# The key maxima of the next pair of heads, queued later on VectorE in a three-stage attention, expert and mixer kernel

## The chip, the cores and the metric

The kernel runs as one program on one core of a Trainium2 chip. The metric is the device time of the whole launch in microseconds (us), as a median of runs. Five engines work from queues of their own, each in the order in which its instructions stand: PE (TensorE, with PEld for its weight loads), DVE (VectorE), ACT (ScalarE), POOL (GpSimd) and SP (SyncE, which issues the loads and stores here). They wait for one another by semaphores.

## The reference, cut to what matters

Three stages follow each other, for two batches of 768 positions:

```python
# stage 1: attention, 8 heads of 64, over a window and over 24 block summaries
k_sum = k.reshape(B, H, nb, block, D).max(axis=3)      # key maxima of blocks of 32
v_sum = v.reshape(B, H, nb, block, D).mean(axis=3)
scores_l = np.where(mask_l, scale * q @ k.T, -1e9)     # |i - j| < 16
scores_s = scale * einsum(q, k_sum) + np.log(block)
a = softmax(concat(scores_l, scores_s)); attn = a @ concat(v, v_sum)
...
# stage 2: four experts of causal attention (q, k, v by x @ w), the best two per position weighted
# stage 3: mixer over positions (w_tok1, w_tok2), then over channels
h2 = np.maximum(u @ w_ch1, 0.0) @ w_ch2                # 512 -> 1536 -> 512
return u + h2
```

The mixer's weights come as 64-bit floats and are decoded on the chip.

## The kernel before, in words

**Stage 1, batch by batch, pair by pair.** Heads go in pairs (`hp`, four a batch), a pair's 768 positions in three groups `g` of four tiles of 64 queries. `s1_load` loads a pair's keys `kx` (already cut into windows, with 24 free columns a tile for the key maxima), its queries `qb`, its values `vt` and `vx`. `s1_keys` makes the key maxima: a reduction on DVE (L185, tile `km`) and a copy into `kx` (L187). Per group, PE multiplies the scores (`s1_scores`, L217, tile `s1s`), DVE takes the minima of the negated scores (`s1_minima`, L227, tiles `n` and `mn`, four pairs of instructions), ACT exponentiates (L236), POOL and DVE normalise (L240, L244, L252), PE turns the result (L257), ACT copies it out (L262), PE multiplies by the values (L271), and ACT and DVE split the result into a high and a low part (L279, L282). Scores of four tiles take a bank of PSUM; there are three banks of that kind, and a bank comes free when the minima have read it. `sc`, `km` and the others have numbers in an order listing: `s1s102` is batch 1, pair 0, group 2; `kx11` is batch 1, pair 1.

**What sets the order.** Batch 0's stage 1 follows a list written out by hand. Batch 1's (the function `s1`) is written in a loop, and a scheduler places its instructions on each engine, with its own estimate of times, among those that it may run with. `tc.issue_after(x)` keeps what is issued under it behind instruction `x` in its engine's queue, and `last["mn", b, hp, g]` is the last minimum of that group. Both queries buffers serve two pairs in turn, so that the loads of pair `hp + 2` are issued when pair `hp`'s scores are done.

**Around it.** Beside batch 1's stage 1 run the projections of batch 0 (`proj`, tiles `pv`, `pj`, V), then the experts' attention (`attn`: L476 scores, L481 minima, L486 exponentials, L492 the multiplication on POOL, L502 turns, L507 to L513 values), the token mixer (`tokmix`, whose last step makes `u`, split into `u0h` and `u0l`), and the decoding of the mixer's weights (`decode_w`, L140 to L153: a load into one of two buffers `raw`, and steps on ACT, POOL and DVE; tile names `raw`, `deca`, then `t1`, `t2`, `c1`, `c2` with h for high and l for low). The channel mixer (`chmix`, tiles `h` and `o`) takes the second half of the time in four passes; the first needs `u` of batch 0 and the first six decoded channel tiles (`c1` and `c2`, three each).

Of the kernel before, what the change touches and what calls it, by code (L numbers as in the profile page):

```python
# [53 lines left out]
def stack_kernel(ctx: ExitStack, tc, qT, kT, kwT, vw, vT, wqkv, wo, tok1, tok2, ch1, ch2,  # L54
# [4 lines left out]
    last = {}  # L59
# [96 lines left out]
    def s1_load(b, hp, qb):  # L156
        first = b == 0 and hp == 0
        kx = unit([P, NT, KX], F32, f"kx{b}{hp}")
        kt = None
        if first:  # L160

            kt = kt0
            vec.memset(kx[:, 0, KW:KX], 0.0)

        vt = half([P, S], F32, "vt") if b else None
        vx = unit([P, NT, P], F32, f"vx{b}{hp}")
        loads = [(kt, kT) if first else (kx, kwT[b, hp])]
        loads += [(qb[i::2, :, i, :], qT[b, hp, i::2].rearrange("p (t c) -> p t c", c=P)) for i in range(2)]
        if first:
            loads += [(lmask, lmask_d), (ident, ident_d), (blocks, blocks_d)]  # L170
        loads += ([(vt, vT[b, hp])] if b else []) + [(vx[:KW], vw[b, hp])]
        for d, src in loads:
            if b == 0:
                r = tc.keep_in_program_order(nc.sync.dma_start(d, src))
            else:
                with tc.issue_after(last["load"].ins):
                    r = nc.sync.dma_start(d, src)
        last["load"] = r
        return kt, vt, kx, vx

    def s1_keys(kt, vt, kx, vx):
        km = sp1.tile([P, NBLK], F32, name="km")
        sums = (kx[:, :, KW:KX], km[:, None, :].broadcast_to([P, NT, NBLK]))
        if kt is None:
            vec.tensor_reduce(km.rearrange("p (t n) -> p t n", t=NT),  # L185
                              kx[:, :, WIN:WIN + TQ].rearrange("p t (n c) -> p t n c", c=BLK), axis=AX.X, op=ALU.max)
            vec.tensor_copy(*sums)  # L187
            return
        vec.tensor_reduce(km, kt[:, WIN:WIN + S].rearrange("p (n c) -> p n c", c=BLK), axis=AX.X, op=ALU.max)
        kc = kt[:, :S].rearrange("p (t c) -> p t c", c=TQ)  # L190
        w = 4
        for t in range(0, NT, w):
            u = min(t + w, NT - 1)
            vec.tensor_copy(kx[:, t:t + w, 0:TQ], kc[:, t:t + w])
            vec.tensor_copy(kx[:, t:u, TQ:KW], kc[:, t + 1:u + 1, 0:2 * WIN])
            if t + w == NT:
                vec.tensor_copy(kx[:, NT - 1, TQ:KW], kt[:, S:S + 2 * WIN])
            if t == 0:
                vec.tensor_copy(*sums)
# [13 lines left out]
    def s1_scores(b, hp, g, qb, kx):  # L213
        sc = bank("sc", f"s1s{b}{hp}{g}")
        for i in range(4):
            t = 4 * g + i
            ten.matmul(sc[:, KX * i:KX * i + KX], qb[:, t // 2].rearrange("p i c -> p (i c)")[:, t % 2::2], kx[:, t, :],  # L217
                       start=True, stop=True)
        return sc
# [19 lines left out]
    def s1_sm(sm):  # L239
        gps.tensor_scalar(sm, sm, 1e-9, 1.0, op0=ALU.add, op1=ALU.mult)  # L240

    def s1_ri(sm):
        ri = sp1.tile([P, 4], F32, name="ri", bufs=4)
        vec.reciprocal(ri, sm)  # L244
        return ri
# [106 lines left out]
    def s1(xh, xl, qbs):  # L352

        b = 1
        n = 3 * HP
        nq = len(qbs)
        lds = [s1_load(b, 0, qbs[0])]
        ex, pTs, av = {}, {}, {}
        with tc.issue_after(last["mn", 0, HP - 1, 2].ins):
            s1_keys(*lds[0])  # L360
        for i in range(n + 4):
            hp, g = divmod(i, 3)
            if i < n:
                sc = s1_scores(b, hp, g, qbs[hp % nq], lds[hp][2])
                ex[i] = s1_exps(*s1_minima(b, hp, g, sc))
                if g == 0 and len(lds) < min(hp + 2, HP):
                    lds.append(s1_load(b, hp + 1, qbs[(hp + 1) % nq]))
            if 0 <= i - 1 < n:
                pr, sm = ex[i - 1]
                s1_sm(sm)  # L370
                s1_mul(b, pr, s1_ri(sm))
            if i < n and g == 1:
                with tc.issue_after(last["mn", b, hp, 0].ins):
                    vs = s1_sums(*lds[hp])
                s1_means(b, hp, vs, lds[hp][3])
                if hp + 1 < HP:
                    s1_keys(*lds[hp + 1])
            if 0 <= i - 2 < n:
                pTs[i - 2] = s1_turned(s1_turn(b, *divmod(i - 2, 3), ex[i - 2][0]))
            if 0 <= i - 4 < n:  # L380
                s1_low(*divmod(i - 4, 3), av[i - 4], xh, xl)
            if 0 <= i - 3 < n:
                hp, g = divmod(i - 3, 3)
                av[i - 3] = s1_values(b, hp, g, lds[hp][3], pTs[i - 3])
                s1_high(hp, g, av[i - 3], xh)
            if i < n:
                yield
# [275 lines left out]
    lds = []  # L663
# [127 lines left out]
```

## Time and profile before

| | |
|---|---|
| median of 3 runs | 469.67 us (468.07 to 472.2) |
| the profiled execution's own time | 467.73 us |
| its span | 465.9 us |
| PE busy | 445.1 us (96%) |
| DVE, ACT, POOL busy | 280.1, 231.2, 285.2 us |
| granted TensorE clock, mean | 0.998 of full speed |

The profiled execution took 1.83 us more than its span and lies 1.94 us below the median of the runs. Busy times are sums over stages that differ: what a stage is limited by is read from the idle time of the engines in that stage and from what ended it.

### The profile page before, as it was taken

The numbers are of one execution on the slowest core, as the hardware profiler recorded it, in microseconds if no ns is written. First come the engines' busy times: TensorE is split into PE (matmuls) and PEld (weight loads), VectorE is DVE, ScalarE is ACT, GpSimd is POOL, SyncE is SP. The second block draws the span as 40 slices with busy tenths as digits, with TensorE's granted clock in tenths as the row PEclk, the third lists the DMA queues.
The fourth block names the chain that finished last, engine by engine and source line by source line (L and its number), as shares of the span: only waits on it lengthen the run. The fifth ranks groups of instructions, "written<-read, shape, count | busy, mean of one in ns | idle before, by whom it ended". The sixth has DMA issues, their size and how long they took to land.

```text
span 465.9 us, 8565 instructions
## 1 busy us (share of the span) xinstructions
PE 445.1 (96%) x3038; PEld 420.7 (90%) x3038; DVE 280.1 (60%) x818; ACT 231.2 (50%) x653; POOL 285.2 (61%) x319
## 2 busy tenths in 40 slices
PE   7899899999989878999999999999999999999996
PEld 7798789989978766897999999999999999999996
DVE  5573766759699679868773743677572673332322
ACT  4685665977778687885664423233323321111010
POOL 4568542768989887997873869877864771000000
PEclk9999999999999999999999999999999999999999
DMA  7999917806515865021111120212121100001111
GB/s 222 275 255 310 289 39 207 182 2 167 127 46 152 210 171 146 3 91 45 45 47 46 66 70 2 84 53 78 58 91 45 62 32 0 1 0 69 68 70 68
DMA packets 28522, 46.51 MB, mean 100 GB/s; under 512 B 2496, under 2 KB 19648, under 8 KB 28480
## 3 DMA queue, kind: packets, MB, share of 16 engines
q1 hardware_dynamic: 28480, 45.97, 35.2%
q8 instruction: 24, 0.39, 0.4%
q14 instruction: 18, 0.15, 0.1%
HBM read 33.38 MB, written 3.15 MB: 78 GB/s over the span
## 4 chain that ended last, share of the span: by engine, by line
PE 68%; DMA 10%; DVE 7%; POOL 4%; ACT 3%; issue 3%; SPq 3%; DVEq 0%; ACTq 0%; POOLq 0%
PE h L113 7%; PE h L112 7%; PE h L114 7%; PE o L112 7%; PE o L113 7%; PE o L114 7%; DMA kx<-in_kwT_dram 5%; PE s1s L217 4%; PE s1a L271 2%; DMA qb<-in_qT_dram 2%; POOL pr L492 2%; PE u L112 2%; PE pj L112 2%; PE u L113 2%; PE u L114 2%
## 5 line engine op out<-in xcount | busy, mean ns | idle before, releaser
L144 POOL TENSOR_SCALAR deca<-deca 128x512 f32<-128x512 f32 x30 | 58.0, 1938 | 10.5 <-ACT deca L143 9.7
L113 PE MATMUL o<-hl,c2h 128*128 128x384 f32 x192 | 64.2, 337 | 0.0
L114 PE MATMUL o<-hh,c2l 128*128 128x384 f32 x192 | 64.0, 336 | 0.0
L108 ACT ACTIVATE hh<-h 128x384 fp32r<-128x384 f32 x48 | 23.3, 490 | 79.4 <-PE h L114 78.8
L109 DVE SCALAR_TENSOR_TENSOR hl<-h,hh 128x384 fp32r<-128x384 f32 x48 | 26.5, 555 | 53.2 <-ACT hh L108 53.2
L605 DVE TENSOR_TENSOR oa<-o,oa 128x384 f32<-128x384 f32 x64 | 31.9, 550 | 38.5 <-PE o L114 38.5
L112 PE MATMUL o<-hh,c2h 128*128 128x384 f32 x192 | 49.4, 336 | 0.0
L236 ACT ACTIVATE pr<-n,mn 128x120 f32<-128x120 f32 x96 | 36.6, 384 | 16.3 <-DVE mn L227 15.8
L150 POOL TENSOR_TENSOR raw<-raw 128x512 f32<-128x512 f32 x30 | 31.3, 1042 | 20.4 <-DVE raw L147 18.6
L492 POOL TENSOR_SCALAR pr<-pr,f,wg 128x128 f32<-128x128 f32 (+5 forms) x48 | 40.1, 849 | 5.1 <-DVE f L489 2.9
L151 POOL TENSOR_TENSOR deca<-deca,raw 128x512 f32<-128x512 f32 x30 | 40.8, 1360 | 1.0
L149 ACT ACTIVATE raw<-raw 128x512 f32<-128x512 uint32 x30 | 20.3, 677 | 36.3 <-DMA raw<-in_ch_dram 25.6
L145 DVE TENSOR_SCALAR deca<-deca 128x512 int32<-128x512 int32 x30 | 27.8, 928 | 14.9 <-POOL deca L144 14.9
L486 ACT ACTIVATE pr<-pr,mn 128x128 f32<-128x128 f32 (+5 forms) x48 | 31.9, 665 | 9.8 <-DVE mn L481 9.7
L113 PEld LDWEIGHTS o<-hl,c2h 128*128 128x128 f32 x192 | 36.0, 188 | 0.3 <-DVE hl L109 0.3
L114 PEld LDWEIGHTS o<-hh,c2l 128*128 128x128 f32 x192 | 36.0, 188 | 0.0
L112 PEld LDWEIGHTS o<-hh,c2h 128*128 128x128 f32 x192 | 34.8, 188 | 0.1
L113 PE MATMUL h<-u0l,c1h 128*128 128x384 f32 x96 | 32.5, 338 | 0.0
L112 PE MATMUL h<-u0h,c1h 128*128 128x384 f32 x96 | 32.4, 338 | 0.0
L114 PE MATMUL h<-u0h,c1l 128*128 128x384 f32 x96 | 32.3, 337 | 0.0
L112 PE MATMUL h<-u1h,c1h 128*128 128x384 f32 x96 | 32.3, 336 | 0.0
L113 PE MATMUL h<-u1l,c1h 128*128 128x384 f32 x96 | 32.3, 336 | 0.0
(207 smaller groups left out, 1315.1 us busy)
## 6 DMA issues: line engine op xcount, KB each, us to landing
raw<-in_ch_dram SPq DMA_DIRECT2D x24, 512.0 KB, 3.5
kx<-in_kwT_dram SPq DMA_DIRECT2D x7, 720.0 KB, 10.0
vx<-in_vw_dram SPq DMA_DIRECT2D x8, 576.0 KB, 11.1
qb<-in_qT_dram SPq DMA_DIRECT2D x16, 192.0 KB, 8.9
raw<-in_tok_dram SPq DMA_DIRECT2D x6, 512.0 KB, 4.6
out_dram<-oa SPq DMA_DIRECT2D x16, 192.0 KB, 2.0
vt<-in_vT_dram SPq DMA_DIRECT2D x4, 384.0 KB, 10.3
rqk<-in_wqkv_dram SPq DMA_DIRECT2D x4, 256.0 KB, 10.2
```

What stands on the lines that cost most here:

```text
L109: vec.scalar_tensor_tensor(lo, src, 0.0, hi.bitcast(F32), op0=ALU.max, op1=ALU.subtract)
L112: ten.matmul(out, lh, rh, start=start, stop=False)
L113: ten.matmul(out, lh, rl, start=False, stop=False)
L114: ten.matmul(out, ll, rh, start=False, stop=stop)
L144: gps.tensor_scalar(af, af, F64_TINY, F64_HUGE, op0=ALU.max, op1=ALU.min)
L145: vec.tensor_scalar(ta, ta, 3, 0x3FFFFFFF, op0=ALU.logical_shift_left, op1=ALU.bitwise_and)
L150: gps.tensor_mul(lf, lf, ef)
L151: gps.tensor_add(af, af, lf)
L236: act.activation(pr[:, i, :], n[:, i, :], AF.Exp, bias=mn[:, i:i + 1], scale=-1.0, accum_out=sm[:, i:i + 1])
L486: act.activation(prs[r], prs[r], AF.Exp, bias=mn[:, r, ci:ci + 1], scale=-1.0, accum_out=sm[:, r:r + 1])
L492: gps.tensor_scalar(prs[r][:, :nk], prs[r][:, :nk], f[:, r:r + 1], wg[:, 3 * h + r, e:e + 1], op0=ALU.mult, op1=ALU.mult)
L605: vec.tensor_add(oa[d], a[:, :HALF], oa[d])
```

## The change: where the key maxima of the next pair may stand

In batch 1, `s1_keys` of the next pair is issued in the middle of a pair's second group. It was free to stand anywhere in DVE's queue from there; now its reduction and its copy are kept behind the last minimum of the second group of the pair at work. Nothing is added or taken away, and the first pair of batch 1 has a call of its own, which is as it was.

```diff
                 s1_means(b, hp, vs, lds[hp][3])
                 if hp + 1 < HP:
-                    s1_keys(*lds[hp + 1])
+                    with tc.issue_after(last["mn", b, hp, 1].ins):
+                        s1_keys(*lds[hp + 1])
```

Since the scheduler places everything by estimated times, the order of later work moves too. Lines after L376 have numbers higher by one in the changed kernel.

DVE, batch 1, pair 0 (`s1s100` and `s1s101` are the scores of its groups 0 and 1, `kx11` the keys of pair 1, `wqk1l` a weight of the projections):

```order
 L244 RECIPROCAL ri_622<-sm_602 128x4
-L185 TENSOR_REDUCE km_833<-kx11_749 128x24
 L227 ISA n_737,mn_738<-s1s100_732,lmask_77 128x120
...
 L227 ISA n_807,mn_808<-s1s101_802,lmask_77 128x120
 L227 ISA mn_808 128x1
+L185 TENSOR_REDUCE km_833<-kx11_749 128x24
 L126 TENSOR_TENSOR wqk1l_114<-rqk1_118,wqk1h_113 128x256 x3
+L187 COPY kx11_749<-km_833 128x12x24
```

The reduction of pair 1's keys stood ahead of the minima of groups 0 and 1 of pair 0, and stands behind both now. The same holds for pairs 2 and 3 (`kx12` goes from ahead of the minima of pair 1's groups 0 and 1 to behind both, `kx13` from ahead of group 1's of pair 2 to behind them).

POOL, in the experts' attention of batch 1, between the multiplications of the third expert's first half (`pr384_2983`) and second half (`pr512_3085`); `deca_2813`, `deca_2966` and `deca_3070` are the second, third and fourth channel tile in decoding. Before:

```order
L492 TENSOR_SCALAR pr384_2983<-pr384_2983,f2_2980,wg_1961 128x384
L151 TENSOR_TENSOR deca_2966<-deca_2966,raw64_2965 128x512
L150 TENSOR_TENSOR raw64_3069<-raw64_3069 128x512
L488 TENSOR_SCALAR sm2_3083<-sm2_3083 128x3
L153 TENSOR_TENSOR c1l0_2730<-deca_2966,c1h0_2729 128x512
L151 TENSOR_TENSOR deca_3070<-deca_3070,raw64_3069 128x512
L492 TENSOR_SCALAR pr512_3085<-pr512_3085,f2_3084,wg_1961 128x512
```

The same place on POOL in the changed kernel:

```order
L493 TENSOR_SCALAR pr384_2983<-pr384_2983,f2_2980,wg_1961 128x384
L144 TENSOR_SCALAR deca_2966<-deca_2966 128x512
L151 TENSOR_TENSOR deca_2813<-deca_2813,raw64_2812 128x512
L489 TENSOR_SCALAR sm2_3083<-sm2_3083 128x3
L153 TENSOR_TENSOR c1l0_2730<-deca_2813,c1h0_2729 128x512
L493 TENSOR_SCALAR pr512_3085<-pr512_3085,f2_3084,wg_1961 128x512
```

At this multiplication the decoding of the channel weights stands one tile further back than before: six of its POOL steps (L144 once, L150 twice, L151 twice, L153 once) that stood ahead of `pr512_3085` stand behind it.

SP, at the load of the second channel tile (`raw64_2812`; the `k211` and `k2l11` rows are the copies of the experts' keys of batch 1, which wait for the last projection). Before:

```order
L140 DMA raw64_2733<-in_ch1_dram 128x4x256
L140 DMA raw64_2812<-in_ch1_dram 128x4x256
L449 DMA k211_2253<-s111h_2394 64x768
L450 DMA k211_2253<-s111h_2394 64x768
L453 DMA k2l11_2254<-s111l_2395 64x768 x2
```

And in the changed kernel:

```order
L140 DMA raw64_2733<-in_ch1_dram 128x4x256
L450 DMA k211_2253<-s111h_2394 64x768
L451 DMA k211_2253<-s111h_2394 64x768
L454 DMA k2l11_2254<-s111l_2395 64x768 x2
L450 DMA k211_2253<-s111h_2394 64x768
L451 DMA k211_2253<-s111h_2394 64x768
L454 DMA k2l11_2254<-s111l_2395 64x768 x2
L140 DMA raw64_2812<-in_ch1_dram 128x4x256
```

The second channel tile's load has gone behind the eight copies of keys.

## Rows read from the trace of the kernel before

**Rows 1.** Chain of waits: start us, us, what

```profile
36.42 9.97 DMA kx<-in_kwT_dram
```

**Rows 2.** DVE's instructions in order of time, 46 to 63 us

```profile
46.41 0.95 DVE L185 TENSOR_REDUCE km<-kx 128x24 f32<-128x768 f32 x1 [5.82 <-DMA kx<-in_kwT_dram]
47.28 0.27 DVE L227 CUSTOM_DVE_ANT_0 n<-s1s,lmask 128x120 f32<-128x120 f32 x1
...
48.95 0.30 DVE L187 COPY kx<-km 128x288 f32<-128x288 f32 x1
...
51.26 0.27 DVE L227 CUSTOM_DVE_ANT_0 n<-s1s,lmask 128x120 f32<-128x120 f32 x1
...
62.43 0.95 DVE L185 TENSOR_REDUCE km<-kx 128x24 f32<-128x768 f32 x1 [1.49 <-DMA kx<-in_kwT_dram]
```

**Rows 3.** PE's instructions in order of time, 40 to 84 us

```profile
40.97 1.20 PE L217 MATMUL s1s<-kx,qb 128*128 128x120 f32 x8
...
44.85 1.09 PE L217 MATMUL s1s<-kx,qb 128*128 128x120 f32 x8
48.23 0.50 PE L217 MATMUL s1s<-kx,qb 128*128 128x120 f32 x2 [2.29 <-DVE mn L227]
...
54.02 0.73 PE L217 MATMUL s1s<-kx,qb 128*128 128x120 f32 x4 [0.36 <-DVE mn L227]
...
60.62 0.38 PE L217 MATMUL s1s<-kx,qb 128*128 128x120 f32 x2
...
64.64 1.20 PE L217 MATMUL s1s<-kx,qb 128*128 128x120 f32 x8 [0.95 <-DVE mn L227]
...
75.51 1.09 PE L217 MATMUL s1s<-kx,qb 128*128 128x120 f32 x8
...
79.79 1.09 PE L217 MATMUL s1s<-kx,qb 128*128 128x120 f32 x8
...
83.58 0.39 PE L217 MATMUL s1s<-kx,qb 128*128 128x120 f32 x2
```

**Rows 4.** Stretches: busy PE, PEld, DVE, ACT, POOL; clock, DMA share, GB/s

```profile
36.00:48.00 12.00, 9.94 (x106) 8.76 (x104) 3.97 (x15) 5.20 (x22) 10.48 (x17) 1.00 1.05 304
48.00:64.00 16.00, 15.09 (x175) 14.02 (x175) 10.46 (x49) 10.22 (x44) 6.95 (x17) 1.00 0.78 219
...
250.00:300.00 50.00, 50.00 (x287) 49.48 (x287) 25.17 (x43) 17.71 (x34) 40.39 (x33) 1.00 0.13 43
```

**Rows 5.** The sum of the stretches from 102 to 230 us

```profile
sum 128.00, PE 118.68 PEld 104.24 DVE 105.31 ACT 97.66 POOL 111.88; mean PE 9.13 PEld 8.02 DVE 8.10 ACT 7.51 POOL 8.61
```

**Rows 6.** Loads issued at 35.24 and 74.45 us: KB, us to landing

```profile
vt<-in_vT_dram SPq DMA_DIRECT2D x1, 384.0 KB, 7.1
...
kx<-in_kwT_dram SPq DMA_DIRECT2D x1, 720.0 KB, 6.0
```

**Rows 7.** POOL's decoding steps by line: count, busy us, mean ns, idle before

```profile
L144 POOL TENSOR_SCALAR deca<-deca 128x512 f32<-128x512 f32 x30 | 58.0, 1938 | 10.5 <-ACT deca L143 9.7
...
L150 POOL TENSOR_TENSOR raw<-raw 128x512 f32<-128x512 f32 x30 | 31.3, 1042 | 20.4 <-DVE raw L147 18.6
...
L151 POOL TENSOR_TENSOR deca<-deca,raw 128x512 f32<-128x512 f32 x30 | 40.8, 1360 | 1.0
```

**Rows 8.** DVE's decoding steps by line, 100 to 240 us: same columns

```profile
L146 DVE SCALAR_TENSOR_TENSOR deca<-raw,deca 128x512 int32<-128x512 int32 x14 | 12.2, 869 | 0.1
...
L145 DVE TENSOR_SCALAR deca<-deca 128x512 int32<-128x512 int32 x14 | 10.1, 721 | 2.8 <-POOL deca L144 2.8
...
L147 DVE TENSOR_SCALAR raw<-deca 128x512 int32<-128x512 int32 x14 | 8.8, 627 | 0.0
```

**Rows 9.** Tile `c2l`: ns min/median/max, first and last start, shapes

```profile
L114 PEld LDWEIGHTS o<-hh,c2l x192: 187/188/192, 243.1 to 461.5; 128*128 128x128 f32 x192
...
L153 POOL TENSOR_TENSOR c2l<-deca,c2h x12: 1284/1297/1418, 208.9 to 385.7; 128x512 fp32r<-128x512 f32 x12
```

**Rows 10.** POOL in order of time: the third `c2l` step of the first six tiles

```profile
228.49 1.28 POOL L153 TENSOR_TENSOR c2l<-deca,c2h 128x512 fp32r<-128x512 f32 x1
```

## The prediction

> **What bounds the kernel now.** I read the stretches first: how long PE stands idle in each, since from 250 to 300 us it works without a pause [rows 4], and the end moves by what the time before that loses or wins. From 36 to 64 us, about the stretch that the change touches, PE is idle for 2.06 + 0.91 = 2.97 us of 28 [rows 4]; from 102 to 230 us for 9.32 of 128 [rows 5]. So PE is nearly the bound there already. Then PE in order of time: three pauses, 2.29, 0.36 and 0.95 us, the last from 63.69 to 64.64, make up all of it (2.29 + 0.36 + 0.31 up to 64), and each ended with a minimum on DVE [rows 3]. Then DVE in order of time, for why the minima were late: from 40.6 to 46.41 us it waited 5.82 us for the keys of pair 1, with nothing left ahead of that pair's key maxima; only then came the minima of pair 0's group 0, whose scores PE had finished at 40.97 + 1.20 = 42.17 us [rows 2, 3]. The chain of waits shows the same load, 9.97 us long, as a piece of its own [rows 1]. The reader is to see a wait for something needed later that stands in front of something needed now.
>
> **The 2.29 us pause.** Moved behind the minima of group 1, the reduction no longer holds group 0 back: its minima start at 42.2 instead of 47.28 us. They read the scores and free a bank of PSUM at about 43, before PE finishes group 1's scores at 45.94 [rows 3], so PE goes on with group 2 at once. Does another wait take over? Next on DVE stands a sum over `vt`, loaded at 35.24 us and landed 7.1 us later, at 42.3 [rows 6]: no wait. From the first minimum of group 0 to that of group 1 DVE took 3.98 us [rows 2]; started at 42.2, it comes to group 1 at 46.2, just after its scores, and four minima of 0.27 us end at 47.0 to 47.3. The reduction follows, and its keys landed at 46.41 [rows 2]: it waits for nothing. Sum: -2.29 us.
>
> **The 0.36 and 0.95 us pauses.** Both are waits for minima that stood behind the same stall or behind the next one. The second is pair 1's: its group 0 minima stood behind the reduction of pair 2's keys, which waited 1.49 us and started at 62.43 [rows 2]; PE needed their bank at 63.69 and got it at 64.64 [rows 3]. After the change PE reaches that point 2.65 us sooner, at 61.04; group 0's last scores, 60.62 + 0.38 before, are done at 58.35, and four minima later it is 59.4. Both pauses go: -1.31 us.
>
> **What is late next.** The loads of pair 2 are issued when pair 0's scores are done, and in the new order two of the last four products stand further back on PE, so that these loads leave at about the time they left before. Nor would leaving sooner help: the DMA share is 1.05 from 36 to 48 us [rows 4], so a load joins a full line. I leave `kx12` landing at 62.4. Its reduction now stands behind pair 1's group 1 minima: PE starts those scores at 61.04, they take 1.20, minima 1.1, so it starts at 63.3 and waits for nothing. The first user, pair 2's group 0, is at 75.5 before, 71.9 then [rows 3]: the reduction (0.95 us) and its copy have over 7 us of cover. Pair 3 is the tight one. Its load follows the copies of the projections, which PE brings 3.6 us sooner; 6.0 us of landing [rows 6] puts the keys at 76.9 instead of 80.4. The reduction then waits for pair 2's group 1: scores 79.79 + 1.09 - 3.6 = 77.3, minima to 78.2, reduction to 79.2, copy (0.30 [rows 2]) to 79.5; PE wants the keys at 83.58 - 3.6 = 80.0 [rows 3]. The cover there is 0.5 us, and every microsecond beyond it would be a microsecond on PE. I cost it at nothing. Sum of the stage: **-3.6 us**.
>
> **What is carried to the end.** PE, POOL, DVE and ACT all start the next stage that much sooner, and no load there stands at a fixed time. But the scheduler has also dealt the work from 102 to 230 us anew, and that stretch is mixed: PE 93%, POOL 87%, DVE 82% busy [rows 5]. Two moves bear on it, both counted in instructions that stand ahead of something that PE needs.
> - Decoding of the channel weights goes back. Ahead of the first split of `u`, with which the channel mixer's stretch begins, one tile's three DVE steps less: 0.72 + 0.87 + 0.63 = 2.2 us [rows 8]; ahead of a later one, two tiles' (4.4) less and one step of 0.5 more, net 3.9. On POOL 1.94 + 2 x 1.04 + 2 x 1.36 + 1.30 = 8.0 us less ahead of the multiplication shown [rows 7, 9]. The gain's end: 3.9, what DVE gives up, since the split needs DVE whatever POOL does.
> - In batch 0's attention it goes the other way: ahead of the third expert's first minima, one decoding tile's DVE steps (2.2) and seven smaller ones, some 1.8 us by their neighbours, come in. The loss's end: +4.0.
>
> No row shows how such moves come out: work taken out from ahead of a step shortens its wait only while its engine is what it waits for. I take **-0.9 us**, 40% of the 2.2 at the first split, nearer to the gain because that place is the last one before PE is full. Total -4.5 us, with ends of -3.6 - 3.9 = -7.5 and -3.6 + 4.0 = +0.4.
>
> **A rule on how much room there is.** The room that I read from PE's busy time, 9.3 us from 102 to 230 us, is a ceiling on what the second stage can give [rows 5]. The Trainium skill, "Perfetto Trace Analysis", section "Identifying the Most-Contended Engine", says that matmul busy time is no good measure of how near TensorE is to its limit, since matmuls are pipelined, and that the busy share of weight loads is to be used. By that measure the room there is 128 - 104.24 = 23.8 us; the trace bears the rule out, for in the full stretch the weight loads are busy for 49.48 of 50 us [rows 4, 5]. By that measure the first rival below would be nowhere near the ceiling: its 3.9 us are 42% of the 9.3, and 16% of the 23.8.
>
> **Rivals.**
> - *The second stage gains in full.* Everything that DVE gives up at the later split of `u` is gained: -3.6 - 3.9 = -7.5 us, 462.2 us as a median. For it: decoding stood between attention's steps on all three engines and needs only to be ready for the channel mixer. Against: batch 0's attention gets decoding in front.
> - *The gain is given back.* Attention of batch 0 meets its 4.0 us on DVE, or pair 3's keys are late, and the 3.6 us are spent by 230 us: 467 to 471, say 469.7 us. This is also what would come if the stall only changed its name, so that DVE waits for a landing behind another instruction.
> - *Slower: the channel tiles come too late.* Their decoding has gone back, and the second tile's load has gone behind eight copies. Before, the third low half of `c2` was ready at 228.49 + 1.28 = 229.8 us, and PE took up the first at 243.1 [rows 9, 10], 13.3 us of cover; with PE 4.5 us sooner it is 8.8. The three came from 208.9 to 228.5, 9.8 us apart [rows 9, 10]. One place back costs 9.8 and is nearly all covered; 8.0 us of POOL is 1.4 tiles of 5.6; at two places the tile is ready at 249.4 where PE wants it at 238.6, a wait of 10.8 against a gain of 4.5: +6.3, 476.0 us. It decides from 8.8 us of delay and ends slower than before from 13.3. Against it: the next six tiles keep their place on POOL, so the first six have to catch up before them.
>
> **How the numbers follow.** The profiled execution took 467.73 us; less 4.5 that is 463.2. The median of the runs is 1.94 above it, so I forecast 469.67 - 4.5 = **465.2 us** as a median. About 1% (4.7 us) is what a measurement of this kernel can tell from no change; the forecast lies just inside. Chances: the forecast, -2.5 to -5.5 us, 0.45; the full gain, beyond -5.5, 0.25; given back, -2.5 to +1.5, 0.20; slower, beyond that, 0.10. Faster by over 1% is all of the second and somewhat under a third of the first: 0.38. Slower by over 1% is some half of the last: 0.06. Between: 0.56. For 8 times in 10 the range leaves out the slower case and the far end of the full gain: -8.2 to +1.2 us, 461.5 to 470.9.
>
> **What would show it.** Right: the wait of L185 for the keys is gone from DVE for pairs 1 to 3, or falls, for pairs 1 and 2 together, from 7.3 us (5.82 + 1.49) to under 1; PE has no pause at a score product between 45 and 65 us; the third group of pair 2 and what follows on PE stand 3.6 us earlier. The second stage is right if PE's idle time from 102 to 230 us, shifted, falls by a microsecond or so. Wrong: a pause of PE of over 0.5 us before pair 3's scores; a wait for `vt` on DVE; PE waiting for `c2l`; or PE's idle time growing after 102 us by as much as it fell before.

## The result, and the profile after

The changed kernel is slower: 471.94 us (20 runs) against 468.79 (20 runs of the kernel before on the same chip). The ratio is 1.0071 with a 95% interval of 1.0049 to 1.0094, so 3.3 us (2.3 to 4.4) more. I had forecast 4.5 us less. The profiled execution took 473.46 us, its span is 471.7, the mean granted clock 0.978; the 20 runs granted 0.973 to 0.996. The ratios here and below are of undisturbed executions, and km_rest, whose profiled execution was a disturbed one, has no row in the table of starts and no line of its trace shown.

What the edit aims at came about. VectorE's instructions in order of time in the changed kernel, the three key maxima of pairs 1 to 3 with a minimum ahead and two copies:

```profile
49.38 0.27 DVE L227 CUSTOM_DVE_ANT_0 n<-s1s,lmask 128x120 f32<-128x120 f32 x1
...
49.58 0.94 DVE L185 TENSOR_REDUCE km<-kx 128x24 f32<-128x768 f32 x1
...
52.35 0.30 DVE L187 COPY kx<-km 128x288 f32<-128x288 f32 x1
...
64.94 0.95 DVE L185 TENSOR_REDUCE km<-kx 128x24 f32<-128x768 f32 x1
...
80.04 0.95 DVE L185 TENSOR_REDUCE km<-kx 128x24 f32<-128x768 f32 x1
81.02 0.78 DVE L187 COPY kx<-km 128x288 f32<-128x288 f32 x1
```

The waits of 5.82 and 1.49 us in front of the first two [rows 2] are gone: none of the three has a bracket. The stretches of the same kernel (busy PE, PEld, DVE, ACT, POOL, then granted clock, DMA share, GB/s):

```profile
36.00:48.00 12.00, 12.00 (x138) 10.77 (x135) 7.74 (x32) 8.19 (x34) 10.63 (x16) 1.00 1.03 321
48.00:64.00 16.00, 16.00 (x190) 15.35 (x189) 11.73 (x57) 11.46 (x51) 10.21 (x25) 1.00 0.76 225
...
82.00:102.00 20.00, 20.00 (x213) 16.89 (x212) 10.33 (x58) 15.04 (x59) 11.18 (x30) 1.00 0.39 79
102.00:230.00 128.00, 118.49 (x701) 105.58 (x700) 101.88 (x289) 93.62 (x240) 96.83 (x100) 0.95 0.39 101
230.00:250.00 20.00, 18.12 (x115) 16.62 (x115) 14.38 (x27) 12.37 (x28) 18.89 (x17) 1.00 0.17 54
250.00:300.00 50.00, 50.00 (x296) 49.43 (x295) 26.65 (x47) 18.08 (x36) 41.34 (x34) 1.00 0.16 53
```

From 36 to 64 us PE is busy throughout, where it had stood idle for 2.97 us [rows 4]. The loss is hard to see in busy times. From 102 to 230 us PE is idle for 9.51 us, against 9.32 before [rows 5], and for 1.88 more up to 250. What stands out is the clock: 0.95 of full speed over 128 us, with 1.00 before and after. PE in order of time, the pauses over 1.5 us from 140 to 200 us:

```profile
154.39 0.53 PE L477 MATMUL s2s<-k,q 128*128 128x128 f32 x2 [2.26 <-DVE s110l L105]
...
175.08 0.33 PE L536 MATMUL yt<-ident,yT 128*128 128x128 f32 x1 [1.58 <-DVE mn L482]
...
189.53 0.52 PE L513 MATMUL s2a<-ph,V 128*128 128x384 f32 x1 [2.59 <-ACT ph L104]
```

And the stretches behind each:

```profile
154.00:158.00 4.00, 2.91 (x12) 2.37 (x13) 2.44 (x9) 3.95 (x11) 2.41 (x3) 0.70 1.01 226
158.00:162.00 4.00, 4.00 (x15) 3.30 (x14) 2.90 (x9) 2.07 (x6) 0.67 (x2) 0.50 1.03 254
...
176.00:180.00 4.00, 4.00 (x15) 3.03 (x14) 3.86 (x7) 3.01 (x8) 3.33 (x5) 0.57 0.99 272
...
190.00:194.00 4.00, 3.59 (x18) 2.98 (x18) 4.00 (x12) 3.44 (x9) 1.99 (x3) 0.60 0.00 0
```

At 158 us PE is busy for all 4.00 us, at a granted clock of 0.50, the lower level of 1.2 GHz, and gets 15 products done. So in this execution each of the three pauses is paid once as idle time and again as busy time at half speed, for some 14 us in all. That second price does not follow from the length of the pause: pair3, a kernel further down, has the first of these pauses too, at the same place, and keeps its clock behind it:

```profile
153.66 0.52 PE L477 MATMUL s2s<-k,q 128*128 128x128 f32 x2 [2.31 <-DVE mn L482]
```

and the stretch behind that:

```profile
154.00:158.00 4.00, 3.36 (x21) 2.64 (x21) 2.91 (x12) 3.95 (x13) 1.63 (x3) 1.00 1.00 238
```

To follow this through many kernels I compare when the same instructions start, in us against the trace of the kernel before: the first low half `x0l` (22.2 us there; it is ahead of all that differs, so this column is only the scatter between executions), the last `x1l` (103.1; stage 1 is done), the last low half of `u0` (233.4; PE is full from here), the last output `oa` (462.3).

| kernel | `x0l` | `x1l` | `u0l` | `oa` | between `x1l` and `u0l` |
|---|---|---|---|---|---|
| changed | +2.7 | +0.1 | +5.8 | +5.8 | 5.7 lost |
| km_only | -0.3 | -4.7 | -4.3 | -3.4 | 0.4 |
| front_after | -1.0 | -3.6 | -3.2 | -3.2 | 0.4 |
| rest_after | -1.8 | -2.5 | +2.9 | +2.8 | 5.4 |
| s1a_whole | -0.2 | -3.9 | -3.8 | -4.0 | 0.1 |
| early1760 | -1.9 | -5.4 | -0.5 | +0.1 | 4.9 |
| late1760 | 0.0 | -4.4 | -2.2 | -1.6 | 2.2 |
| loads_paired | -0.9 | -5.4 | +1.6 | +3.1 | 7.0 |
| km_whole | -1.9 | -5.6 | -5.4 | -4.5 | 0.2 |
| pair12 | -1.5 | -4.4 | -4.4 | -4.5 | 0.0 |
| pair3 | -1.6 | -0.3 | +5.8 | +5.7 | 6.1 |

The changed kernel's first column is a lower clock from 12 to 24 us (0.72 there), ahead of the edit, in the one execution that was profiled. rest_after has the front of before and still stands 0.7 us lower in its second column than in its first, so differences of a microsecond between two rows are scatter. From `x0l` on the changed kernel gains 2.7 - 0.1 = 2.6 us up to `x1l`, and then loses 5.7.

### The profile page after: what moved, and what is told of

Its sections match the earlier page's. It is cut to its first block, busy times and chain, and to the rows that moved or that the text cites. A ratio compares the mean times of both kernels' runs of the same rounds, so it can differ in the third digit from the quotient of the medians.

```text
span 471.7 us, 8573 instructions
## 1 busy us (share of the span) xinstructions
PE 452.4 (96%) x3038; PEld 427.4 (91%) x3038; DVE 286.2 (61%) x818; ACT 230.4 (49%) x653; POOL 283.3 (60%) x319
## 4 chain that ended last, share of the span: by engine, by line
PE 80%; DVE 6%; DMA 5%; POOL 4%; ACT 2%; issue 2%; SPq 1%; DVEq 0%; ACTq 0%; POOLq 0%
PE o L112 7%; PE o L113 7%; PE o L114 7%; PE h L113 7%; PE h L114 7%; PE h L112 7%; PE s1s L217 4%; PE s1a L271 3%; PE s2s L477 3%; PE vm L293 3%; PE s1p L257 3%; DMA raw<-in_ch_dram 2%; PE u L112 2%; PE u L113 2%; PE u L114 2%
## 5 line engine op out<-in xcount | busy, mean ns | idle before, releaser
L144 POOL TENSOR_SCALAR deca<-deca 128x512 f32<-128x512 f32 x30 | 58.1, 1940 | 19.8 <-ACT deca L143 19.2
L150 POOL TENSOR_TENSOR raw<-raw 128x512 f32<-128x512 f32 x30 | 31.6, 1055 | 21.2 <-DVE raw L147 18.5
L493 POOL TENSOR_SCALAR pr<-pr,f,wg 128x128 f32<-128x128 f32 (+5 forms) x48 | 37.4, 788 | 6.0 <-PE s2p L503 3.1
L151 POOL TENSOR_TENSOR deca<-deca,raw 128x512 f32<-128x512 f32 x30 | 40.1, 1337 | 1.3
L145 DVE TENSOR_SCALAR deca<-deca 128x512 int32<-128x512 int32 x30 | 30.4, 1014 | 13.9 <-POOL deca L144 13.9
L503 PE MATMUL s2p<-ident,pr 128*128 128x128 f32 x168 | 31.3, 286 | 1.6 <-DVE u0l L105 1.2
```

The lines of the kernel that those rows point to most:

```text
L144: gps.tensor_scalar(af, af, F64_TINY, F64_HUGE, op0=ALU.max, op1=ALU.min)
L145: vec.tensor_scalar(ta, ta, 3, 0x3FFFFFFF, op0=ALU.logical_shift_left, op1=ALU.bitwise_and)
L150: gps.tensor_mul(lf, lf, ef)
L151: gps.tensor_add(af, af, lf)
L493: gps.tensor_scalar(prs[r][:, :nk], prs[r][:, :nk], f[:, r:r + 1], wg[:, 3 * h + r, e:e + 1], op0=ALU.mult, op1=ALU.mult)
L503: ten.transpose(pT[:, P * r:P * r + P], prs[r][:, P * j:P * j + P], ident)
```

## The experiments

**How an order is held.** The scheduler places instructions anew whenever an edge is added. To change one thing and keep the rest, most kernels here are the kernel before with this call at the end, where `ORDER` lists for each engine the instructions in the order wanted:

```diff
+def in_order(tc, rows):
+    at = {x.name: x for x in tc.nc.cur_bb.bb.instructions}
+    for row in rows:
+        row = [n for n in row if n in at]
+        for a, x in zip(row, row[1:]):
+            if at[a].engine == at[x].engine:
+                tc.add_manual_dep(at[x], a, NOSYNC, reason="keep_in_program_order")
 ...
     psa_cm.__exit__(None, None, None)
+    in_order(tc, unpack(ORDER))
```

These are edges of issue order, as `issue_after` makes them, and the computation is the same in every kernel. Where a kernel follows one order up to a point and the other behind it, the point is a place in the scheduler's single list of all 4296 instructions. In their rows, lines stand 63 further down: L280 is L217 of the kernel before, L539 its L476. Differences in us are the ratio's, with its 95% interval, times the median of the kernel before on the same chip (467.29 to 468.33).

**1. The six instructions alone (km_only).** In `ORDER`, on VectorE:

```diff
-km<-kx11 (ahead of pair 0's group 0 minima)
-kx11<-km (between the minima of groups 0 and 1)
 n,mn<-s1s101 (four minima of pair 0's group 1)
+km<-kx11, kx11<-km
 ...   (the same for kx12 behind s1s111 and kx13 behind s1s121)
```

> The order of the kernel before is kept on every engine by edges of issue order, except that the six instructions of the key maxima (three reductions, three copies) stand behind the fourth minimum of the second group, where the change puts them; nothing later is dealt anew. Theory A (the two pauses before pairs 1 and 3 go, the loss of the change comes from the work that the scheduler dealt anew behind it): 3.6 us less than the kernel before (bounds 2 to 4.5), no pause of TensorE from 45 to 65 us. Rival B (the moved maxima themselves give the gain back, because the third groups or the next pair wait longer): the time of the kernel before within 1 us. Rival C (the result is a matter of the clock from run to run, not of any order): also within 1 us of the kernel before.

Measured: ratio 0.9941 (0.9914 to 0.9968), 2.8 us less (1.5 to 4.0). The stretches of its profile:

```profile
48.00:64.00 16.00, 16.00 (x172) 15.30 (x172) 11.28 (x57) 11.83 (x48) 9.25 (x20) 1.00 0.71 210
...
82.00:102.00 20.00, 20.00 (x206) 18.12 (x207) 11.69 (x54) 16.25 (x57) 13.07 (x26) 1.00 0.20 46
102.00:230.00 128.00, 118.29 (x724) 103.77 (x724) 103.08 (x290) 96.16 (x243) 112.64 (x112) 1.00 0.41 110
```

The clock keeps its level from 102 to 230 us, with PE about as busy as in the changed kernel. Theory A holds, B and C fall: moving the maxima gains by itself, and 4.3 of the 4.7 us that the table shows at `x1l` are still there at `u0l`, and 3.4 at the last output.

**2 to 4. One order in front, the other behind (front_after, rest_after, cut1600).** `ORDER` is the changed kernel's up to the last product of stage 1, then that of before; the reverse; and the first with the point at instruction 1600.

> The order of the changed kernel up to the last local product of batch 1 (about 102 us), the order of the kernel before from there on, on every engine, fixed by edges of issue order. Theory A with all of the loss behind 102 us: 2 to 4 us less than the kernel before. If about 2 us of the gain are given back by the changed order of the products at 85 to 102 us (relative to the offset at the start, the trace of the changed kernel shows 4.6 us gained at 64 us and 2.6 at 102), 1 to 2.6 us less. Rival B: the time of the kernel before, or up to 2 us more. Rival C: within 1 us of the kernel before.

> The order of the kernel before up to the last local product of batch 1, the order of the changed kernel from there on: the pauses before pairs 1 and 3 are kept and the later work stands as the change deals it. Theory A: the loss without the gain, 5 to 7 us more than the kernel before (the change's own 3.3 us more, plus the 2.6 to 3.6 us that the front no longer gives), with pauses of TensorE of 1.5 us and more between 146 and 195 us. Rival B: within 1 us of the kernel before, since the front's order is that of before. Rival C: within 1 us.

> As the kernel with the changed order up to 102 us, but with the changed order kept to instruction 1600 of 4296 (about 143 us), and the order of before from there on. Theory A with the loss at 146 to 195 us (where the changed kernel's trace has new pauses of TensorE of 2.26, 1.58 and 2.59 us): the same as the kernel that keeps the changed order to 102 us, within 1 us. If the loss is at 102 to 143 us: 3 us or more above that kernel. Rivals B and C: as for that kernel.

Measured: front_after 0.9964 (0.9938 to 0.9991), 1.7 us less (0.4 to 2.9); rest_after 1.012 (1.0069 to 1.017), 5.6 us more (3.2 to 8.0); cut1600 1.0035 (1.0004 to 1.0066), 1.6 us more (0.2 to 3.1). Gain and loss can be had apart, and they add up: -1.7 + 5.6 = +3.9, where the change itself is +3.3. The loss lies behind 102 us and needs nothing of the front. cut1600 does not settle where: it came out 3.3 us above front_after, as a loss between 102 and 143 us would have it, but PE pauses 2.15 us in it up to 141.31, at the joint of the two orders, and neither the changed kernel nor the kernel before has that pause.

**5. Whole blocks of products (s1a_whole).** front_after's table, with four blocks on PE put together, as here:

```diff
-L320 MATMUL s1p_1358<-ident,pr 120x128
-L334 MATMUL s1a_1366<-pTs,vx_948 64x64
-L320 MATMUL s1p_1358<-ident,pr 120x128
-L334 MATMUL s1a_1366<-pTs,vx_948 64x64 x2
-L320 MATMUL s1p_1358<-ident,pr 120x128
-L334 MATMUL s1a_1366<-pTs,vx_948 64x64
-L320 MATMUL s1p_1358<-ident,pr 120x128
-L334 MATMUL s1a_1366<-pTs,vx_948 64x64 x4
+L320 MATMUL s1p_1358<-ident,pr 120x128 x4
+L334 MATMUL s1a_1366<-pTs,vx_948 64x64 x8
```

> As the kernel with the changed order up to 102 us and the order of before behind it (1.7 us less than the kernel before), but on TensorE each block of eight 64 by 64 products s1a stands whole again: the changed order has three of batch 1's blocks (s1a120, s1a121, s1a131) cut into pieces by transposes s1p and one more (s1a111) is cut in both kernels. Theory D (a block in one piece costs less: 112 products are busy 4.8 us at 78 to 104 us where the blocks are whole and 6.3 us where they are cut): 1 to 1.7 us less than with cut blocks, 2.7 to 3.4 us less than the kernel before. Rival E (the cutting costs nothing, the 2 us are given back by something else in the front's order): 1.7 us less than the kernel before, as with cut blocks.

Measured: 0.9944 (0.9913 to 0.9976), 2.6 us less (1.1 to 4.1), where cut blocks gave 1.7 less (0.4 to 2.9); the two intervals overlap, so the times alone don't tell. The stretch from 82 to 102 us for tile `s1a` alone (PE, PEld, DVE, ACT) does, in front_after, where the blocks are cut:

```profile
82.00:102.00 20.00, 5.63 (x96) 3.98 (x96) 2.96 (x7) 2.27 (x6) 1.00 0.20 48
```

and in s1a_whole:

```profile
82.00:102.00 20.00, 4.11 (x96) 3.28 (x96) 2.95 (x7) 2.61 (x7) 1.00 0.24 56
```

The same 96 products keep PE busy for 5.63 us when cut and 4.11 whole: 1.52 us. By the trace theory D holds. This is what the changed order gives back in front: kernels with its front gain 2.5 or 2.6 us between `x0l` and `x1l`, eight with the maxima moved alone 3.0 to 4.5. The products of a block write to the two halves of the output's partitions in turn. The Trainium skill, "TensorE: Matmul & The Clock Gate", section "Part 3: Packing small matmuls — row/col tiling", says that products at different places of the array run at the same time; 43 ns a product in whole blocks and 59 in cut ones fit that, but no run here separates it from other reasons for the difference.

**6 to 8. Is it the decoding? (km_rest, decode_late, decode_early)** km_rest has km_only's order up to 102 us and the changed one behind. decode_late has km_only's order, but with each of the 308 decoding instructions put behind as many of PE's products as in the changed order; decode_early has km_rest's order with the decoding where the kernel before has it.

> Up to the last local product of batch 1 the order of before with the six key-maxima instructions moved alone (as in the kernel that gained 2.8 us), from there on the order of the changed kernel on every engine. Theory A (front and later work add up): the gain of 2.8 us and the loss of 5.6 us together, 2 to 3.5 us more than the kernel before. Rival F (the loss depends on where the front leaves off, since the same later order meets other times): 0 to 1 us or over 4.5 us more.

> The order of before with the six instructions moved, all else as before, except that the decoding of the weights (loads of raw, the steps on ScalarE, VectorE and GpSimd, 308 instructions from the second t2 tile on) is put back to where the changed kernel has it, counted in products of TensorE. Theory G (the decoding that is put back by 80 to 160 instructions is the loss behind 150 us: its loads block the loads of k behind them on SP, its ScalarE steps stand in front of attention's): 2 to 3.5 us more than the kernel before. Rival H (the loss comes from the other work that was dealt anew, batch 1's projections and the loads of q and k behind them): 2 to 3.5 us less than the kernel before, as with the maxima moved alone.

> The reverse: the order of before with the six instructions moved up to 102 us, from there the order of the changed kernel, but the decoding of the weights where the kernel before has it, ten products later. Theory G: 2 us or more less than the kernel before; the pauses of TensorE of 1.6 and 2.3 us at 170 to 190 us are gone. Rival H: 2 to 3.5 us more than the kernel before, with these pauses. Both in part: near the kernel before, the first pause (2.25 us at 150 us) staying and the two later ones gone.

Measured: km_rest 1.0043 (1.001 to 1.0077), 2.0 us more (0.5 to 3.6): front and rest add up (-2.8 + 5.6), F falls. decode_late 1.0229 (1.0181 to 1.0278), 10.7 us more; decode_early 1.02 (1.0153 to 1.0246), 9.3 more. Neither G nor H is borne out, and the question itself falls: either kernel is far worse than both orders that it is mixed from, so a mix of this kind does not tell the share of each. decode_late has new waits of PE for ScalarE, the largest in order of time:

```profile
215.59 0.45 PE L575 MATMUL s2a<-ph,V 128*128 128x384 f32 x1 [2.20 <-ACT ph L167]
...
232.92 0.59 PE L575 MATMUL s2a<-ph,V 128*128 128x384 f32 x1 [2.83 <-ACT ph L167]
```

Which decoding step stands between which steps of attention, on four queues at once, is worth 10 us here.

**9 and 10. The rest in two halves (early1760, late1760).** km_only's order, but the changed one from 102 us to instruction 1760 (about 151 us), or from there on. At this point the two orders differ by five instructions on either side, so the joint adds little.

> The six instructions moved alone up to 102 us, the order of the changed kernel from there to instruction 1760 of 4296 (just behind the first scores s2s of batch 1's selected attention, about 151 us), the order of before behind that. Theory J (4.3 of the 5.5 us that the changed order loses behind 102 us come at that point: the second split of s100h is later, the loads of q from it leave as half, other half, half, other half, ScalarE's split s110h waits for them, VectorE's s110l for that, TensorE 2.25 us for its bank, and its clock is granted at half for some 10 us after): 1 to 2 us more than the kernel before. Rival K (the loss is the decoding put back behind that point): 2 to 3.5 us less than the kernel before.

> The other half: the order of before with the six instructions moved up to instruction 1760, the order of the changed kernel behind it, with all of the decoding that it puts back by 80 to 160 instructions. Theory J: 1 to 2 us less than the kernel before (2.8 gained, 1.2 lost). Rival K: 1 to 3 us more than the kernel before, with the pauses of 1.4 and 2.3 to 2.9 us of TensorE at 170 and 185 us as in the changed kernel.

Measured: early1760 1.0014 (0.9987 to 1.004), 0.7 us more (-0.6 to 1.9); late1760 1.0007 (0.9975 to 1.0039), 0.3 us more (-1.2 to 1.8). Against km_only each loses about 3 us, and in the table 4.9 and 2.2; their sum, 7.1, is near the 7.0 of loads_paired, which has both halves (the changed kernel and rest_after lose 5.7 and 5.4 there). So the loss lies in both halves. In the first J holds and K falls. For the second the time lies between what J and K say, and the later pauses that K asks for are there. ScalarE in order of time in early1760 shows how the first half loses:

```profile
138.60 0.40 ACT L549 ACTIVATE pr<-pr,mn 128x128 f32<-128x128 f32 x1 [2.67 <-DVE mn L544]
...
140.61 0.47 ACT L167 ACTIVATE s100h<-pj 128x384 fp32r<-128x384 f32 x1
...
146.24 0.87 ACT L167 ACTIVATE s110h<-pj 128x384 fp32r<-128x384 f32 x2 [1.06 <-DMA q<-s100h]
```

and in km_only:

```profile
139.98 0.49 ACT L167 ACTIVATE s100h<-pj 128x384 fp32r<-128x384 f32 x1 [0.15 <-PE pj L177]
...
144.53 0.49 ACT L167 ACTIVATE s110h<-pj 128x384 fp32r<-128x384 f32 x1
```

In km_only the split `s100h` follows its products at once. In the changed order it waits behind exponentials that wait 2.67 us for minima (VectorE works on batch 1's gates, L476 to L492, between 132.0 and 138.0 us and starts these minima at 138.28; in km_only part of the gates stands behind them and they start at 133.72). The loads of `q` leave later, the first at 141.10 instead of 140.50 us, and the next split into the same buffer waits 1.06 us for them. PE in order of time in early1760, at the end of this:

```profile
148.92 0.87 PE L539 MATMUL s2s<-k,q 128*128 128x128 f32 x2 [2.28 <-DVE s110l L168]
```

The granted clock is 0.50 in early1760 from 150 to 155 us, with 18 products in these 5 us, and 1.00 in km_only, with 31. In late1760 the pauses are 1.40 us (166 us), 2.79 (180 us) and 1.25 (226 us), and from 180 to 185 us the clock is 0.66.

**11, 13 and 14. Mending that pause (loads_paired, split_first, split_paired).** One exchange on SP in km_rest's order; one on ScalarE in early1760's; both there.

```diff
 (SP: loads_paired, split_paired)
-L512 DMA q_1963<-s100h 64x768
-L513 DMA q_1963<-s100l 64x768
-L512 DMA q_1963<-s100h 64x768
-L513 DMA q_1963<-s100l 64x768
+L512 DMA q_1963<-s100h 64x768 x2
+L513 DMA q_1963<-s100l 64x768 x2
 (ScalarE: split_first, split_paired)
+L167 ACTIVATE s100h<-pj_2053 128x384
 L549 ACTIVATE pr_2372,sm_2370<-pr_2372,mn_2369 128x128
 L549 ACTIVATE pr_2373,sm_2370<-pr_2373,mn_2369 128x256
 L215 ACTIVATE t2h<-deca 128x2x256
 L549 ACTIVATE pr_2374,sm_2370<-pr_2374,mn_2369 128x384
-L167 ACTIVATE s100h<-pj_2053 128x384
```

> As the kernel with the six instructions moved alone up to 102 us and the changed order behind it (2.0 us more than the kernel before), with one exchange: on SP both loads of q from s100h stand ahead of both from s100l, as in the kernel before. Theory J with the order of these loads as the larger part of the wait: ScalarE's wait for q from s100h of 1.05 us falls to 0.5 or less, TensorE's pause at 151 us from 2.2 to 1.6 or less, the time 0 to 1.4 us above the kernel before. Rival L (the late split of s100h alone makes the wait): pause and time as without the exchange, 2 us more than the kernel before.

> As the kernel with the changed order from 102 us to instruction 1760 and the order of before elsewhere (0.65 us more than the kernel before, TensorE's pause at 149 us 2.28), with one exchange on ScalarE: the second split s100h stands ahead of the three exponentials of s2s0300, behind which the changed order has it. Theory M (its place behind exponentials that wait for minima makes the pause): s100h starts 2 us earlier, ScalarE's s110h waits under 0.4 us for the loads of q, TensorE's pause is under 1 us and the clock keeps its level, 1.5 to 3 us less than the kernel before. Rival N (the pause comes from elsewhere, s110h or VectorE late anyway): pause over 1.7 us, time within 1 us of the kernel before.

> As the one with s100h ahead, and on SP both loads of q from s100h ahead of both from s100l. Theory M with the second load of s100h held back by the one of s100l in front of it: the pause goes from between 1 and 1.7 us (with s100h ahead alone) to under 0.9, 2 to 3 us less than the kernel before. If s100h's place is the whole: as the kernel with s100h ahead alone, within 0.8 us. Rival N: pause over 1.7 us.

Measured: loads_paired 1.0057 (1.0027 to 1.0087), 2.7 us more (1.3 to 4.1), pause 2.08. Pause and time come out as L says, but not for L's reason: ScalarE's `s110h` does not wait for the loads any more, as J says, and VectorE's `s110l` waits 1.88 us for those from `s100l` instead. split_first 1.0013 (0.9993 to 1.0033), 0.6 us more; split_paired 1.0003 (0.9972 to 1.0033), 0.1 more; both as early1760. Theory M falls and N's signs are met in split_first: its pause is again 2.28 us, ScalarE still waits 1.14 us for the loads from `s100h`, and VectorE 2.19 for those from `s100l`. In split_paired ScalarE no longer waits for the loads, but VectorE does, in order of time:

```profile
147.37 0.56 DVE L168 TENSOR_TENSOR s110l<-pj,s110h 128x384 fp32r<-128x384 f32 x1 [1.37 <-DMA q<-s100l]
```

and PE has two pauses for one:

```profile
148.92 0.53 PE L539 MATMUL s2s<-k,q 128*128 128x128 f32 x2 [1.37 <-DVE mn L544]
...
154.12 0.45 PE L576 MATMUL s2a<-pl,V 128*128 128x384 f32 x1 [2.00 <-DVE pl L168]
```

The low half `s100l` stands behind decoding on VectorE (L208 to L210, up to 142.28 us) just as the high half stood behind exponentials on ScalarE. With one link mended the next comes last, and the time stays. That the low half's place is the rest of the cause is read from these waits; no run moved it.

**12. A version that beats both (km_whole).** km_only, with the one block that both kernels cut (`s1a111`) whole.

```diff
-L334 MATMUL s1a_1282<-pTs,vx_751 64x64 x3
 L271 MATMUL vm_1266<-ident,vs 24x128
 L320 MATMUL s1p_1274<-ident,pr 120x128 x4
-L334 MATMUL s1a_1282<-pTs,vx_751 64x64 x5
+L334 MATMUL s1a_1282<-pTs,vx_751 64x64 x8
```

> The order of before with the six instructions moved, and on TensorE the one block of eight products s1a that both kernels cut (s1a111, three and five around four transposes and one mean) made whole. If a whole block costs less, as the kernel with the whole blocks suggests (three blocks made whole: 2.3 us less at 102 us in the trace): 0.3 to 0.8 us less than the kernel with the maxima moved alone, 3 to 3.6 us less than the kernel before. If not: 2.8 us less.

Measured: 0.9917 (0.9888 to 0.9946), 3.9 us less (2.5 to 5.2). Against km_only the intervals overlap, so the block's own worth is not shown.

**15 and 16. The edit for some pairs, dealt by the scheduler (pair12, pair3).** No order is held here.

```diff
-                    with tc.issue_after(last["mn", b, hp, 1].ins):
+                    with tc.issue_after(last["mn", b, hp, 1 if hp < 2 else 0].ins):
                         s1_keys(*lds[hp + 1])
```

(pair3 has `hp == 2` for `hp < 2`.)

> The scheduler's own order, with the edit made for pairs 1 and 2 alone; pair 3's key maxima are queued behind the minima of the first group instead. What it deals differs from the kernel before at 63 places of TensorE's queue (the change itself: 793). Theory A (the front gains, a new deal of the later work loses): 2.29 and 0.36 us of pauses gone, pair 3's 0.95 us kept, hardly anything dealt anew: 1.5 to 3 us less than the kernel before. Rival B (the change gains nothing of itself): within 1 us of the kernel before.

> The scheduler's own order, with the edit made for pair 3 alone; those of pairs 1 and 2 are queued behind the first group's minima. What it deals differs from the changed kernel at 120 places of TensorE's queue and from the kernel before at 817. Theory A: the loss of the new deal, with 0.95 us of gain at most: 4 to 6 us more than the kernel before, pauses at 150, 170 and 185 us as in the changed kernel. Rival B: 0 to 3.3 us more, as the changed kernel or less.

Measured: pair12 0.9914 (0.9887 to 0.994), 4.0 us less (2.8 to 5.3); pair3 1.0134 (1.01 to 1.0168), 6.3 us more (4.7 to 7.9). My expectation of pair12 gave the 0.95 us pause to pair 3; it is pair 1's scores behind pair 2's keys [rows 2, 3], and it is gone here too. pair12's stretches:

```profile
48.00:64.00 16.00, 16.00 (x174) 15.29 (x174) 12.39 (x59) 12.09 (x54) 10.60 (x25) 1.00 0.83 225
...
82.00:102.00 20.00, 20.00 (x211) 18.05 (x208) 12.69 (x62) 17.74 (x65) 14.26 (x31) 1.00 0.22 54
102.00:230.00 128.00, 118.75 (x727) 104.22 (x726) 103.48 (x291) 96.66 (x243) 112.96 (x112) 1.00 0.41 110
```

and pair3's:

```profile
82.00:102.00 20.00, 20.00 (x211) 17.02 (x208) 10.32 (x56) 15.09 (x58) 11.00 (x29) 1.00 0.32 81
102.00:230.00 128.00, 117.11 (x708) 104.52 (x707) 101.89 (x291) 93.18 (x239) 98.62 (x101) 0.97 0.38 101
```

Theory A holds, and the loss has one origin: the edge for the maxima of pair 3. pair12 and the changed kernel differ in the text by that edge alone (behind the first group's minima, where the kernel before had these maxima anyway, or behind the second's), and lie 7.3 us apart: 4.0 less and 3.3 more. Queueing pairs 1 and 2 later removes the three pauses of the front and leaves the scheduler's later order nearly as it was. Queueing pair 3's later removes no pause, since none stood there [rows 3], and makes the scheduler deal the rest anew; pair3's stretches have the changed kernel's marks, 17.02 us of weight loads from 82 to 102 us and POOL's 98.62 from 102 to 230. (pair3 also holds pair 1's and 2's maxima to the first group's minima, and that front has pauses of its own, so not all of its 6.3 us is the new deal: the table shows 6.1 us lost behind `x1l`.)

## Why the prediction was wrong

**The 2.29 us pause; the 0.36 and 0.95 us pauses.** Right, and in size: 3.6 us forecast, 2.8 (1.5 to 4.0) measured as a time with the rest held fast, and 3.0 to 4.5 us between `x0l` and `x1l` in eight traces with that front. Only the 0.36 us pause is not always gone: four of these eight traces have no pause there, and four one of 0.18 to 0.61 us. PE in order of time in early1760:

```profile
49.88 0.73 PE L280 MATMUL s1s<-kx,qb 128*128 128x120 f32 x4 [0.61 <-DVE mn L290]
```

The moved reduction and its copy now stand ahead of the minima of group 2, for which this product of pair 1 waits; the prediction did not ask what the six instructions would hold back in their new place.

**What is late next.** Right for the keys: no wait for `vt`, none for `kx`. Pair 3's cover was put at 0.5 us; in the changed kernel its copy ends at 81.02 + 0.78 = 81.80, the 24 score products that need it start at 82.76, 0.96 us later, and PE doesn't pause. But this step ended with "Sum of the stage: -3.6 us", and the changed order gives 2.6 in the trace, 1.7 in time: it cuts three more blocks of `s1a`. PE is busy throughout 82 to 102 us in both, so its busy time could not warn of it; its weight loads show it, 16.89 us in the changed kernel and 18.12 in km_only, 16.98 in front_after and 18.14 in s1a_whole.

**What is carried to the end.** This is the step that failed. "PE, POOL, DVE and ACT all start the next stage that much sooner" and carry it holds for an order left alone (km_only, pair12: 0.4 and 0.0 us lost). The scheduler's new deal I took at -0.9 us, with ends of -3.9 and +4.0. It measured +5.6 us (3.2 to 8.0, rest_after), past the worse end by its middle value. I had counted instructions put ahead of or behind a step and multiplied by their durations. What decided was which instruction stood behind a waiting one. The pause at 150 us stands at neither of the two places that I priced. Around the third expert's first minima of batch 0 (126 us in the changed kernel) PE's longest pause is 0.52 us; the one at 150 us begins, as early1760 shows it, with ScalarE's wait for the fourth expert's minima, and comes through two splits, a buffer that loads still read, and four queues. And I left out the second price that a pause can have, the clock. decode_late and decode_early suggest that a count of this kind could not have served: two orders mixed by such counts cost some 10 us each.

**The rivals.** "The gain is given back" comes nearest, its sign and its check ("PE's idle time growing after 102 us by as much as it fell before") half right: PE's idle time from 102 to 250 us grew by 2.07 us, and the rest of the 5.7 us lies in busy time, some 14 us of it at the lower clock. Its price, 469.7 us, was too low. The time fell where I had put the slower rival, beyond +1.5 us, but not by that rival's mechanism: no pause of PE for `c2l` is in the trace. That the second stage gains in full was wrong in sign.

**The rule on room.** PEld's 23.8 us of room against PE's 9.3 was no forecast of gain; with 105.58 us of weight loads instead of 104.24 [rows 5] the changed kernel shows neither room used nor lost.

**What stays open.** Which of the steps that the changed order moves makes the 2.2 us lost behind 151 us, whether moving both halves of the split forward on both engines would close the pause at 150 us, and why the clock falls behind some pauses and not behind others as long; none of these was tried.

## What to carry to other kernels

An edge that removes a wait is worth what its own place in the trace says only if the scheduler leaves the rest alone: look at how much of every queue changes, and if much does, hold the old order and move just the instructions meant. Put the edge only where a pause stands: here two of its three uses gain 4.0 us, and the third, with nothing to gain, brings the time to 3.3 us above the kernel before. When an order is dealt anew, look for waiting instructions with splits and loads queued behind them, and allow for the clock that a pause of PE may cost behind it as well.

## What the runs showed of the hardware

The granted clock fell to 0.50 (1.2 GHz) behind some pauses of PE: of 2.26, 1.58 and 2.59 us in the changed kernel (to 0.50, 0.57 and 0.60 in the 4 us stretches shown above), of 2.28 in early1760, and of only 1.25 and then 0.41 in late1760 (226 us; 0.60 from 227 to 231). Behind others as long it stayed at 1.00: of 2.29 us in the kernel before [rows 3, 4], 2.15 in cut1600 (141 us), 2.31 and 1.64 in pair3 (154 and 171 us), 1.32 in early1760 (172 us). In rest_after, which has the front of before, it fell behind the very pause that left it at 1.00 there (1.82 us; 0.57 from 47 to 51 us). So here the length of a pause did not decide alone, and what else does is not shown. In early1760, up to `u0l`, one pause of 2.28 us and what followed lost 4.9 us, over twice its length; split_first, with the same length and a shorter stretch at the lower clock, lost 3.6. The Trainium skill, "TensorE: Matmul & The Clock Gate", section "HAM oscillation — how this bites in real kernels", says that a matmul engine that waits too long between groups of products starts the next group at the lower clock; the traces show that behind some of these pauses and not behind others.

Eight 64 by 64 products in a row cost 43 ns each; with transposes between them 59 ns (4.11 and 5.63 us over 96).
